# All seven products by blocks in the last two chunks of a fused attention and SwiGLU kernel

## The chip, the cores and the metric

The kernel runs on one core of a Trainium2 chip. Five engines work side by side, each with its own queue of instructions that it takes in order: TensorE (PE, with its weight loads shown apart as PEld), VectorE (DVE), ScalarE (ACT), GpSimd (POOL), and SyncE (SP), which here only issues transfers. They wait for each other on semaphores. The metric is the device time of one execution in microseconds; lower is better.

## The reference

```python
scores = q @ k.T / sqrt(64)                       # 8 batches x 8 heads, 576 x 576
scores = where(scores >= max(scores) - tau, scores, -1e9)
attn   = softmax(scores);  x = attn @ v           # heads joined: x is 4608 tokens x 512
g, val = x @ w_gate, x @ w_val                    # 512 -> 1536, both
out    = (g * sigmoid(g) * val) @ w_out           # 1536 -> 512
```

All of it is float32.

## The kernel before

**Order.** The program is written out by a planner when it is built (class `Plan`, from line 30). `pe()` appends to TensorE's queue at once, in the order in which the Python code calls it. Work for the other engines is a `job` with an engine, an assumed duration, what it depends on and a rank; the planner places jobs into each engine's queue by the time at which it believes they can start, the lower rank first. So the order within each queue is fixed in the program, by assumed durations; on the chip the semaphores alone decide the times.

**Chunks.** The FFN takes the tokens in nine chunks of 512. Chunk c below 8 is the first 512 tokens of batch c; chunk 8 (`B` in the code) is the last 64 tokens of all eight batches, collected in `last_hbm`. In the *main part* there are 84 slots of attention scores (L1989) with softmax and the attends (L2088); the FFN work of earlier chunks is put between them. Behind the last scores and attends comes the *tail* (from L2321, `tail[0] = True`): chunk 7's gates, chunk 7's outputs, chunk 8's gates, chunk 8's outputs, one after the other.

**Gates and values.** For one chunk the products with `w_gate` and `w_val` are made in six groups g of 256 columns each. In a group, a two-by-two scheme of Winograd's kind replaces eight products by seven, p1 to p7, each of a sum of weight blocks and a sum of token blocks; the results are combined by adds. `Group` (L1092) makes each product with four matmuls of 128x128 weights by 256 tokens (`mul`, L1109). The weights' sums were made once and lie in `sums_hbm`, nine pieces of 512 columns per group, and `load_flow` (L1030) brings a group's pieces into one of two slots, in two transfers of 1280 and 1024 KB, for each chunk anew. `NestedGroup` (L1276) makes two of the seven products, p5 and p3, *by blocks*: the same scheme once more inside the product, seven matmuls of 128x128 by 128 tokens in place of four by 256 (L1294). Such a product leaves seven blocks in two PSUM banks (512 and 384 columns), which have to be copied out and folded by four adds (`Seven.fill` at L1214 and L1216, `Seven.fold`, `fold_banks` at L1233). It also needs four further sums of weights (the pieces 0 and 8 of `sums_hbm`) and four further sums of token blocks (`deepen_x`). In the main part some groups are nested; in the tail all are.

**After the products.** p1's result is copied within PSUM by ACT (`cb`, L1116), so that p2 adds to the one copy and p6 to the other. p6's result goes through ACT to a buffer u1 (L1155), to which p3's is added: the gate for one half. p7's and p5's give the other. `finish` takes a tanh (L1163, ACT), multiplies by the value (L1164, DVE), and multiplies by the gate into `hall`. This last multiply and some sums are POOL's in the main part (helper line L925) and DVE's in the tail (helper line L928).

**Outputs.** `Deep` (L1641) makes the products with `w_out`, nested by blocks (L1711, 21 matmuls each; in the tail some flat ones, L1720). It needs sums of the gated values: `early`, `late` and `inner_sums`; results come through `combine` (L1748 and helper adds) and are stored.

**Weights' slots.** SP issues every load in its queue's order; a load that waits for a slot to be free holds up the ones behind it.

## Time and profile before

| | |
|---|---|
| median of 3 runs (lowest to highest) | 1350.09 us (1348.88 to 1350.68) |
| the profiled execution: its own time | 1349.87 us |
| its span | 1348.0 us |
| granted TensorE clock, mean | 1.00 |
| busy: PE / DVE / ACT / POOL | 1334.6 / 1066.5 / 895.7 / 778.0 us |
| last attends of the main part's scores on TensorE | 1126.1 us |
| tail's gates begin | 1135.6 us |
| HBM read / written | 172.36 MB / 27.13 MB |

The profile's rows name a line of the kernel, an engine, an operation, out<-in by the program's names, the tile's shape, the count, then the busy time in us, the mean of one in ns, and after the bar the idle time ahead of these instructions with what ended it. A float32 matmul stands in the trace as two records, so the counts of PE rows are twice those of the code. `tmp`, `big`, `hall`, `vall`, `pall`, `tall`, `xall`, `obs`, `qT` and `kT` are SBUF tiles, `pa`, `pb`, `pe`, `sc`, `px` and `py` PSUM banks. `big` is a large tile with many uses, weights' slots among them.

### The profile page before, as it was taken

Reading aid. Unit: us, or ns where it says so; the run is one execution under the profiler, and the core shown is the slowest. Engines: PE = TensorE matmul, PEld = TensorE weight load, DVE = VectorE, ACT = ScalarE, POOL = GpSimd, SP = SyncE. Lnnn points to the kernel's source line nnn. Section 1 sums busy time; section 2 is a strip of 40 time slices with the busy share of each in tenths; the row PEclk is TensorE's granted clock in tenths of the full one; section 3 lists DMA queues with packets and bytes.
Section 4 is the critical chain, followed back from the end, with each engine's and each line's share of the span. In section 5 each row is a group of like instructions: output and inputs, shape, how many; then the busy total and the mean of one; then the engine's idle time right before and its main releaser. Section 6 shows DMA issues by size and latency. Waiting matters only on the chain.

```text
span 1348.0 us, 40299 instructions
## 1 busy us (share of the span) xinstructions
PE 1334.6 (99%) x15914; PEld 1118.9 (83%) x15914; DVE 1066.5 (79%) x2860; ACT 895.7 (66%) x2315; POOL 778.0 (58%) x870
## 2 busy tenths in 40 slices
PE   9999999999999999999999999999999999999998
PEld 7777777787888878888888888887888889999998
DVE  7888898888887777888788888888788876586686
ACT  6888777767756677787777777778677773330330
POOL 2677497565685659745994689566965594000000
PEclk9999999999999999999999999999999999999999
DMA  8753324356557543746264636562565518524621
GB/s 178 206 186 96 79 58 133 122 149 177 153 166 225 169 126 92 211 137 203 62 201 145 216 97 195 158 215 69 139 212 145 171 57 270 195 96 165 210 80 32
DMA packets 216140, 202.11 MB, mean 150 GB/s; under 512 B 166800, under 2 KB 184208, under 8 KB 205200
## 3 DMA queue, kind: packets, MB, share of 16 engines
q1 hardware_dynamic: 212032, 198.62, 50.0%
q8 instruction: 126, 2.06, 0.6%
q10 hardware_dynamic: 3920, 0.92, 0.3%
q14 instruction: 62, 0.51, 0.1%
HBM read 172.36 MB, written 27.13 MB: 148 GB/s over the span
## 4 chain that ended last, share of the span: by engine, by line
PE 93%; DVE 2%; DMA 2%; POOL 1%; ACT 1%; issue 1%; SPq 0%; ACTq 0%; DVEq 0%; POOLq 0%
PE pb L1109 19%; PE pa L1109 13%; PE px L1711 12%; PE sc L1989 10%; PE xa L2088 9%; PE pe L1109 6%; PE po L1416 6%; PE pe L1294 4%; PE py L1711 3%; PE pv L1341 2%; PE pg L1341 2%; PE sc L1294 2%; PE py L1720 2%; PE sc L483 1%; PE pv L600 1%; DMA wo<-in_moe_w_gate_dram 1%
## 5 line engine op out<-in xcount | busy, mean ns | idle before, releaser
L2037 DVE SCALAR_TENSOR_TENSOR pall<-sc,th,pall 128x288 f32<-128x288 f32 x504 | 244.3, 513 | 42.0 <-ACT pall L2035 22.6
L1109 PE MATMUL pb<-xall,big 128*128 128x256 f32 x1152 | 273.9, 381 | 0.0
L2035 ACT ACTIVATE pall<-sc,nm 128x288 f32<-128x288 f32 x504 | 232.8, 498 | 33.6 <-DVE pall L2037 33.5
L1109 PEld LDWEIGHTS pb<-xall,big 128*128 128x128 f32 x1152 | 214.9, 190 | 30.7 <-issue 2.7
L2066 DVE STREAM_TRANSPOSE pall<-pall 128x576 f32<-128x576 f32 x252 | 188.4, 764 | 23.6 <-ACT pall L2064 15.6
L2064 ACT ACTIVATE pall<-pall,ri 128x288 f32<-128x288 f32 x388 | 179.0, 527 | 28.4 <-DVE ri L2052 27.5
L1109 PE MATMUL pa<-xall,big 128*128 128x256 f32 x768 | 183.1, 381 | 0.0
L925 POOL TENSOR_TENSOR hall<-hall,tmp 128x512 f32<-128x512 f32 x80 | 102.2, 1280 | 106.5 <-DVE hall L1164 86.0
L1109 PEld LDWEIGHTS pa<-xall,big 128*128 128x128 f32 x768 | 143.2, 190 | 21.7 <-issue 2.5
L2010 DVE TENSOR_REDUCE mx<-sc 128x2 f32<-128x576 f32 x168 | 125.9, 750 | 43.4 <-PE sc L1989 42.8
L925 POOL TENSOR_TENSOR big<-big 128x128 f32<-128x128 f32 (+3 forms) x174 | 129.1, 750 | 44.1 <-ACT big L1216 22.3
L1989 PE MATMUL sc<-kT,qT 64*32 64x288 f32 (+1 forms) x5376 | 144.7, 345 | 1.0 <-DVE pall L2037 1.0
L1989 PEld LDWEIGHTS sc<-kT,qT 64*32 64x32 f32 x5376 | 95.1, 106 | 50.0 <-issue 9.3
L2088 PE MATMUL xa<-pall,vall 64*32 64x288 f32 x4032 | 128.8, 404 | 0.4 <-PE px L1711 0.4
L2088 PEld LDWEIGHTS xa<-pall,vall 64*32 64x32 f32 x4032 | 75.4, 107 | 46.1 <-issue 4.3
L2061 POOL TENSOR_SCALAR pall<-pall,ri 128x288 f32<-128x288 f32 x116 | 58.7, 518 | 71.8 <-DVE ri L2052 70.0
L1109 PE MATMUL pe<-xall,big 128*128 128x256 f32 x384 | 91.4, 381 | 0.0
L2046 ACT COPY sums<-sums 32x6 f32<-32x6 f32 x336 | 66.6, 198 | 30.2 <-DVE pall L2037 26.1
L1163 ACT ACTIVATE vall<-tmp 128x512 f32<-128x512 f32 x96 | 59.9, 627 | 36.8 <-POOL tmp L925 17.3
L1109 PEld LDWEIGHTS pe<-xall,big 128*128 128x128 f32 x384 | 72.4, 190 | 11.1 <-ACT pall L2064 1.1
L2012 DVE TENSOR_REDUCE mx<-sc 128x1 f32<-128x288 f32 x168 | 75.0, 446 | 0.0
L925 POOL TENSOR_TENSOR big<-hall 128x384 f32<-128x384 f32 (+2 forms) x69 | 65.2, 969 | 14.6 <-PE pa L1109 14.5
(290 smaller groups left out, 2629.5 us busy)
## 6 DMA issues: line engine op xcount, KB each, us to landing
big<-sums_hbm SPq DMA_DIRECT2D x42, 1280.0 KB, 6.7
big<-sums_hbm SPq DMA_DIRECT2D x42, 1024.0 KB, 6.9
vall<-in_v_dram SPq DMA_DIRECT2D x112, 144.0 KB, 3.6
sums_hbm<-big SPq DMA_DIRECT2D x36, 256.0 KB, 3.6
out_dram<-big SPq DMA_DIRECT2D x32, 256.0 KB, 3.0
qT<-in_q_dram SPq DMA_DIRECT2D x112, 72.0 KB, 4.0
kT<-in_k_dram SPq DMA_DIRECT2D x112, 72.0 KB, 3.1
wo<-in_moe_w_gate_dram SPq DMA_DIRECT2D x16, 384.0 KB, 3.7
```

The costliest lines, as they stand in the source:

```text
L925: return lambda: nc.gpsimd.tensor_tensor(out=out, in0=a, in1=b, op=op)
L1109: nc.tensor.matmul(ps[:, i], w[:, k_, i * P:(i + 1) * P], x[:, k_, :], start=first and i == k_ == 0, stop=True, skip_group_check=True)
L1294: nc.tensor.matmul(self.es[b_].ap()[:, at_ * P:(at_ + 1) * P], ws[n], xd[o][n], start=b_ not in begun, stop=True, skip_group_check=True)
L1416: nc.tensor.matmul(ps, h(f), w[:, f, :], start=(f == 0), stop=(f == NF2 - 1))
L1711: nc.tensor.matmul(ps, a[:, f, :], ws[n][:, f, :], start=bank_ not in begun, stop=True, skip_group_check=True)
L1989: nc.tensor.matmul(pss[h][(slice(g * G, (g + 1) * G), *part)], qT[hs, col:col + G], kT[hs, c * SH + keys[0]:c * SH + keys[1]], start=True, ...
L2010: rs.append(job("DVE", 0.72, lambda n=n, tile_=tile_: nc.vector.tensor_reduce(out=mx[:, n:n + 2, 0], in_=tile_[:, :, 0:SH], axis=AX.X, op= ...
L2035: ej = job("ACT", 0.42, lambda x=x, n=n: nc.scalar.activation(ps[x], scs[x], AF.Exp, bias=nm[:, n:n + 1]), ej, masks.get((h, u - 1)), rank=0)
L2037: masks[x] = job("DVE", 0.45, lambda x=x, n=n: nc.vector.scalar_tensor_tensor(out=ps[x], in0=scs[x], scalar=th[:, n:n + 1], in1=ps[x], op0 ...
L2064: scaled.append(job("ACT", 0.46, lambda x=x, n=n: nc.scalar.activation(x, x, AF.Copy, scale=ri[:, n:n + 1]), rj, rank=rank))
L2066: seg["turned"].append(job("DVE", 0.72, lambda both=both: nc.vector.transpose(out=both, in_=both), *scaled, rank=rank))
L2088: nc.tensor.matmul(holds[a].ap()[x * G:(x + 1) * G, 0:SH].rearrange("d (i q) -> d i q", q=G), vr[rs, h, j, ds], p[rs, h, :, j, :], start=( ...
```

## The change

In the main part the change adds `store_more`: in each of chunks 2 to 6, for each of the six groups, the four further weight sums of one more product (`MORE`: the chunk, and which product) are made from the slot in which that product's weights lie for the chunk's own use. POOL makes them for groups 0 to 4, DVE for group 5; the place is a part of `hall` that is not in use then, and one store of 256 KB brings them to `more_hbm`. The next load into that slot waits for these adds (`load_flow`), and the gated values of group 5 wait for the store (`finish`). In chunk 6's outputs some ranks change.

In the tail, `NestedGroup` is replaced by class `Whole`: all seven products of every group by blocks, for chunk 7 and chunk 8 in turn, group by group: (7,0), (8,0), (7,1) and so on. Weights lie in ten cells of 512 KB (`load_cell`, two transfers of 256 KB each); each of the 42 cells is loaded once and read by both chunks. `deepen_all` makes the token sums for all seven operands of both chunks, on DVE for three of them and on POOL for four. Four pairs of PSUM banks hold the products. The folds of the gate and the value side's inner sums are POOL's; p2's and p4's results are folded by one ACT copy and four DVE adds (`folded`). Chunk 8's gated values are stored to `hall_hbm` and loaded again as four quarters behind the gates; then come the outputs of chunk 7 and of chunk 8, one directly behind the other.

TensorE's order up to the tail's gates is the same in both programs. In the tail it has 588 matmuls of 128x128 by 128 in `product` for what were 240 by 256 and 168 by 128; the output products are the same in number.

```diff
+    MORE = {2: 0, 3: 1, 4: 3, 5: 6, 6: 4}
+    more_reads, more_stores, more_of_place = {}, {}, {}
+
+    def more_place(g, n):
+        at_ = list(MORE.values()).index(n) * HW
+        return more_hbm[g][:, at_:at_ + HW]
+
+    def store_more(c, g):
+
+        n = MORE[c]
+        if (c, g) in more_reads or (c, g, n // 4) not in loads:
+            return
+        w = flow_part(g % 2, n + 1)
+        place = hall[:, g % 2, NF2 - 1]
+        a11, a12, a21, a22 = (w[:, k_, i * P:(i + 1) * P] for i in range(2) for k_ in range(2))
+        t2, t4, t3, t1 = (place[:, k_, i * P:(i + 1) * P] for i in range(2) for k_ in range(2))
+        deps = loads[c, g, n // 4], more_of_place.get((c, g % 2))
+        tt, eng, took, rank = (pool_tt, "POOL", 0.46, 3) if g < NF2 - 1 else (dve_tt, "DVE", 0.25, 2)
+        j = job(eng, took, tt(t3, a11, a21, ALU.subtract), *deps, rank=rank)
+        j = job(eng, took, tt(t1, a21, a22, ALU.add), j, rank=rank)
+        j = job(eng, took, tt(t2, t1, a11, ALU.subtract), j, rank=rank)
+        more_reads[c, g] = j = job(eng, took, tt(t4, a12, t2, ALU.subtract), j, rank=rank)
+        more_of_place[c, g % 2] = more_stores[g, n] = job("SP", 0.1, lambda: nc.sync.dma_start(
+            out=more_place(g, n).rearrange("p (k f) -> p k f", k=2), in_=place), j, lag=2.0, moves=1.3)
...
+        before = (c, g - 2) if g >= 2 else (c - 1, g + NF2 - 2)
+        if before in more_reads and lo <= MORE[before[0]] + 1 < to:
+            deps = *deps, more_reads[before]
...
+                mv = mv, more_of_place.get((self.c, t))
...
+    def load_cell(N, *deps):
+        if N >= NQ * NF2:
+            return
+        g, n = N // NQ, J[N % NQ]
+        place = cell(N)
+        deps = *deps, stores[g], *plain_stores[g], *nested_stores[g]
+        base = job("SP", 0.5, lambda: nc.sync.dma_start(out=place[:, 0:HW], in_=sums_hbm[g][:, (n + 1) * HW:(n + 2) * HW]),
+                   *deps, lag=1.6, moves=0.9)
+        if n in (2, 5):
+            more = sums_hbm[g][:, 0:HW] if n == 2 else sums_hbm[g][:, (NS_ - 1) * HW:]
+            cell_loads[N] = base, job("SP", 0.5, lambda: nc.sync.dma_start(out=place[:, HW:], in_=more), *deps, lag=1.6, moves=0.9)
+            return
+        cell_loads[N] = base, job("SP", 0.5, lambda: nc.sync.dma_start(out=place[:, HW:], in_=more_place(g, n)), more_stores[g, n], *deps,
+                                  lag=1.6, moves=0.9)
...
+            rank = min(rank, 1) if tail[0] else rank
+            if self.c == B - 1 and not self.in_outputs:
+                tt, eng, took = pool_tt, "POOL", 1.3
-            rank = 0 if o == 1 else 1 if o == 5 or o in (3, 6) and not tail[0] else 2
+            tt, eng, took = (dve_tt, "DVE", 0.55) if tail[0] else (pool_tt, "POOL", 1.0)
+            rank = 0 if o == 1 else 1 if o == 5 or o in (3, 6) and not tail[0] or o in (0, 6) and tail[0] or self.c == B - 2 else 2
...
-                tt, eng, took, less, rank = dve_tt, "DVE", 0.42, 0.29, 0
+                tt, eng, took, less, rank = dve_tt, "DVE", 0.42, 0.29, -1 if self.c == B - 2 else 0
...
-            if self.c < B:
+            if self.c < B - 2:
                 load_flow(self.c + 1, g, part, *deps)
+
+        def free_cells(self, *ks_and_deps):
+            if self.c == B - 2:
+                ks, *deps = ks_and_deps
+                for N in sorted((k_ - FIRST_CELL) % NCELL for k_ in ks):
+                    load_cell(N, *deps)
...
+            if c in MORE:
+                store_more(c, g)
...
+    deps = [j for js in ready_x[B - 1].values() for j in js]
+    deepen_all(B - 1, "DVE", -1, 0, 1, 1, fourths[0][:, 0:1], *ready_x[B - 1][0], attended, last=deps)
+    deepen_all(B - 1, "DVE", -1, 2, 2, 2, fourths[0][:, 1:3], *deps, attended)
+    for n, o in enumerate((5, 6, 1, 3)):
+        deepen_all(B - 1, "POOL", 0, o, 1, 1, fourths[1][:, n:n + 1], *deps, attended)
+    x11, x21, x12, x22, s1, s2, s4 = (bases[B][:, n * HW:(n + 1) * HW] for n in range(NQ))
+    free = [j for b in n_list for j in b.jobs]
+    j1 = job("DVE", 0.62, dve_tt(s1, x21, x22, ALU.add), *last_x, rank=0)
+    j2 = job("DVE", 0.62, dve_tt(s2, s1, x11, ALU.subtract), j1, rank=0)
+    j3 = job("DVE", 0.62, dve_tt(x21, x11, x21, ALU.subtract), j2, rank=0)
+    deepen_all(B, "DVE", 0, 0, 1, 1, None, j3, *free)
+    j4 = job("DVE", 0.62, dve_tt(s4, x12, s2, ALU.subtract), j3, rank=0)
+    deepen_all(B, "DVE", 0, 2, 2, 2, None, j4, x_ready[B, 0])
+    for o in (5, 6, 1, 3):
+        deepen_all(B, "POOL", 0, o, 1, 1, None, j4, *free)
...
+        def product(self, n, both, first, *deps):
+            begun = set() if first else {0, 1}
+            N = NQ * self.g + J.index(n)
+            w, more = (cell(N)[:, x * HW:(x + 1) * HW].rearrange("p (k f) -> p k f", k=2) for x in range(2))
+            a11, a12, a22 = w[:, 0, 0:P], w[:, 1, 0:P], w[:, 1, P:2 * P]
+            t2, t4, t3, t1 = (more[:, k_, i * P:(i + 1) * P] for i in range(2) for k_ in range(2))
+            ws, xd = (a11, a12, t4, a22, t1, t2, t3), x_sets[self.c, X_OF[n]]
+
+            def fn():
+                for x in ORDER:
+                    b_, at_ = AT[x]
+                    nc.tensor.matmul(both.ap(b_)[:, at_ * P:(at_ + 1) * P], ws[x], xd[x], start=b_ not in begun, stop=True,
+                                     skip_group_check=True)
+                    begun.add(b_)
+
+            m = pe(NEST, fn, *deps, *cell_loads[N], x_ready[self.c, X_OF[n]])
+            if self.c == B:
+                load_cell(N + NCELL, m)
+            return m
...
+        def p1(self):
+            self.a = Both("pa")
+            m = self.product(0, self.a, True, *self.a.deps)
+            a, b = self.a, Both("pb", full=True)
+            self.b = b
+            self.cb = [job("ACT", (0.57, 0.46)[x], lambda x=x: nc.scalar.copy(b.ap(x), a.ap(x)), m, *b.deps, rank=0) for x in range(2)]
+
+        def p5(self):
+            self.e = Both("pe")
+            m = self.product(2, self.e, True, *self.e.deps)
+            self.s, _ = s7s[0], s7s.rotate(-1)
+            self.c5 = self.s.fill(self.e.holds, m, 0)
...
+            j = job("ACT", 0.28, lambda: nc.scalar.copy(y[:, 4:5], q0[:, 0:1]), m, *st.jobs, rank=0)
+            j = job("DVE", 0.42, dve_tt(y[:, 0:2], twice(y[:, 4:5]), q0[:, 1:3], ALU.add), j, rank=0)
+            j = job("DVE", 0.42, dve_tt(y[:, 3:5], twice(y[:, 1:2]), q1[:, 1:3], ALU.add), j, rank=0)
+            j = job("DVE", 0.29, dve_tt(y[:, 1], y[:, 3], q0[:, 3], ALU.add), j, rank=0)
+            j = job("DVE", 0.42, dve_tt(y[:, 2:4], twice(y[:, 4:5]), q1[:, 0:2], ALU.add), j, rank=0)
+            both.done(j)
...
+        def p6(self):
+            m = self.product(3, self.b, False, *self.cb)
+            self.u, _ = u1s[0], u1s.rotate(-1)
+            self.u1 = self.u.fill(self.b.holds, m, 0)
...
+            tj = job("ACT", 0.6, lambda: nc.scalar.activation(two(n.ap), u.ap, AF.Tanh), gj, *n.jobs, rank=0)
+            o = st.ap[:, 0:DM]
+            vj = job("DVE", 0.75, lambda: nc.vector.scalar_tensor_tensor(out=o, in0=n.ap, scalar=1.0, in1=o, op0=ALU.add, op1=ALU.mult),
+                     tj, fj, rank=0)
+            n.jobs = [vj]
+            eng = ENDS[c][t]
+            tt, took = (dve_tt, 0.62) if eng == "DVE" else (pool_tt, 1.3)
+            to = hall[:, t, g] if c < B else two(o)
+            mj = job(eng, took, tt(to, two(o), u.ap, ALU.mult), vj, rank=0)
+            u.jobs = [mj]
...
+            last_stores[t, g] = job("SP", 0.5, lambda: nc.sync.dma_start(out=hall_hbm[t, h][:, x * HW:(x + 1) * HW], in_=o), mj,
+                                    lag=2.0, moves=0.9)
...
+            js = [job("DVE", (0.7, 0.55)[x], lambda x=x: nc.vector.scalar_tensor_tensor(
+                out=u[:, x * 4 * P:(4, 7)[x] * P], in0=e.ap(x), scalar=0.5, in1=u[:, x * 4 * P:(4, 7)[x] * P], op0=ALU.mult, op1=ALU.add),
+                m, *self.u1, rank=0) for x in range(2)]
+            e.done(*js)
+            j = self.u.fold(GATE_FOLDS[self.c][0], 0, *js)
+            self.finish(0, self.u, j, self.st, self.fa)
...
+            m = self.product(6, self.b, False, *self.u1)
+            b, s_ = self.b, self.s.place
+            self.u2 = [job("DVE", (0.7, 0.55)[x], lambda x=x: nc.vector.scalar_tensor_tensor(
+                out=s_[:, x * 4 * P:(4, 7)[x] * P], in0=b.ap(x), scalar=0.5, in1=s_[:, x * 4 * P:(4, 7)[x] * P], op0=ALU.mult, op1=ALU.add),
+                m, *self.c5, rank=0) for x in range(2)]
+            self.g2 = self.s.fold(GATE_FOLDS[self.c][1], 1, *self.u2)
+
+        def p4(self):
+            m = self.product(4, self.b, False, *self.u2)
+            st, j = self.folded(self.b, m)
+            self.finish(1, self.s, self.g2, st, j)
...
+    old = None
+    for g in range(NF2):
+        for c in (B - 1, B):
+            new = Whole(c, g)
+            new.p1()
+            if old is not None:
+                new.p5()
+                old.p4()
+            if (c, g) == (B - 1, NF2 - 1):
+                state["deep"] = Deep(B - 1, plan.t + plan.PIPE)
+                state["deep"].early(plan.t + plan.PIPE, True)
+            for fn in (new.p2, new.p6, new.p3, new.p7) if old is not None else (new.p5, new.p2, new.p6, new.p3, new.p7):
+                fn()
+                if (c, g) == (B, NF2 - 1) and fn == new.p2:
+                    state["deep"].late(plan.t + plan.PIPE)
+                if (c, g) == (B, NF2 - 1) and fn == new.p6:
+                    state["deep"].sixth_sums(plan.t + plan.PIPE)
+            old = new
+    state["last_product"] = old.p4
+    begin_outputs(B - 1)
+    out_steps(2)
+    behind = plan.t + plan.PIPE
+    used = [j for b in (*u1s, *s7s, *stages, *n3) for j in b.jobs]
+    for x in ob_jobs[0:2]:
+        x += s7s[0].jobs + s7s[1].jobs + s7s[2].jobs
+    stream(5, True, behind)
+    stream(3, True, behind, *used)
+    for n in range(4):
+        t, h = divmod(n, 2)
+        j = job("SP", 0.1, lambda n=n, t=t, h=h: nc.sync.dma_start(out=last_quarters[n].rearrange("p f n -> p (f n)"), in_=hall_hbm[t, h]),
+                *(last_stores[t, h * (NF2 // 2) + x] for x in range(NF2 // 2)), behind, *used, lag=2.0, moves=2.6)
+        for x in range(NF2 // 2):
+            gated[B, t, h * (NF2 // 2) + x] = j
...
+    final = Deep(B, plan.t + plan.PIPE)
+    out_steps(1)
+    final.in_outputs = True
+    final.early(plan.t + plan.PIPE)
+    while state["run"]:
+        out_steps(1)
+    state["deep"] = final
+    begin_outputs(B)
```

More of the change, by code (lines that the diff above doesn't have):

```diff
@@ L1168, in finish @@
             hold.done(True)
-            tt, eng, took = (dve_tt, "DVE", 0.62) if tail[0] else (pool_tt, "POOL", 1.3)
+            tt, eng, took = pool_tt, "POOL", 1.3
             gated[self.c, t, self.g] = mj = job(eng, took, tt(ht, ht, gb.ap, ALU.mult), vj, rank=rank)
@@ L1676, in late @@
             self.ready["s1"].append(self.sum(self.a21, self.a21, self.a22, ALU.add, n - 1, j3[n - 1], gated[c, 1, NF2 - 1], rank=1))
[L1677 removed]
+            self.ready["s2"] = [self.sum(self.s2, self.a22, self.s3, ALU.subtract, x, j3[x], gated[c, 1, n + x], mark, self.read[1], rank=1) for x in range(n)]
         def sum(self, out, a, b, op, x, *deps, rank=2):
@@ L2159, in gates_and_values @@
         old = None
-        settled[0] = c >= DEEP and not tail[0]
+        settled[0] = c >= DEEP
         while u_bufs[0] is not u_list[0]:
@@ new lines, with __init__, free_at, ap @@
+    class Pair:
+        def __init__(self, banks_, full):
+            self.banks, self.full, self.held = banks_, full, False
+        def free_at(self):
+            return max(b.free_at() for b in self.banks)
+    class Both:
+        def __init__(self, name, full=False):
+            free = [p for p in pairs if not p.held and (p.full or not full)]
+            few = sum(p.full for p in free) == 1 and not full
+            self.pair = min(free, key=lambda p: (p.full and few, max(p.free_at(), plan.t)))
+            self.pair.held = True
+            self.holds = [Hold(b, name) for b in self.pair.banks]
+            self.deps = [d for h in self.holds for d in h.deps]
+        def ap(self, n):
+            return self.holds[n].ap()[:, 0:(4, 3)[n] * P]
+        def done(self, *jobs):
+            for h in self.holds:
+                h.read_by(*jobs)
+                h.done(True)
+            self.pair.held, self.pair.full = False, True
@@ new lines, with seven, plain @@
+    mine = [h.bank for h in state["deep"].x]
+    rest = [b for b in banks if b.fixed is None and b not in mine]
+    others = [b for b in banks if b.fixed is not None]
+    pairs = [Pair(mine, True), Pair(rest, False), Pair(others[0:2], False), Pair(others[2:4], False)]
+    def seven(place, *jobs):
+        b = Seven(place)
+        b.jobs = list(jobs)
+        return b
+    def plain(place, *jobs):
+        b = Buf(place)
+        b.jobs = list(jobs)
+        return b
+    old_tall = [behind, *(j for b in (*u_list, *s_bufs) for j in b.jobs)]
```

233 lines of the change are left out of this document (148 added, 85 removed).

## The prediction

> **What bounds the kernel now.** I read the page's busy shares and slices first, then the chain that ended last, then TensorE's waits, then stretches of the span, then the timeline of the stretch at which the change begins to alter TensorE's order.
>
> ```profile
> PE 1334.6 (99%) x15914; PEld 1118.9 (83%) x15914; DVE 1066.5 (79%) x2860; ACT 895.7 (66%) x2315; POOL 778.0 (58%) x870
> POOL 2677497565685659745994689566965594000000
> PE 93%; DVE 2%; DMA 2%; POOL 1%; ACT 1%; issue 1%; SPq 0%; ACTq 0%; DVEq 0%; POOLq 0%
> ```
>
> TensorE is busy 99% and is 93% of the chain: only fewer TensorE microseconds, or a new stall, can move the time. POOL does nothing in the last six slices. The stretches (time, length, then busy and count of PE, PEld, DVE, ACT, POOL, then clock, DMA share, GB/s):
>
> ```profile
> 500.00:700.00 200.00, 200.00 (x2869) 169.25 (x2875) 162.40 (x468) 148.93 (x405) 156.34 (x171) 1.00 0.52 151
> 1150.00:1200.00 50.00, 50.00 (x291) 45.61 (x290) 33.23 (x67) 18.27 (x34) 0.00 (x0) 1.00 0.51 174
> 1300.00:1348.00 48.00, 44.49 (x321) 41.99 (x320) 33.99 (x69) 6.62 (x14) 0.00 (x0) 0.99 0.09 23
> ```
>
> Main part and tail both run with TensorE full. The only waits that TensorE shows after 130 us are of 1.0, 0.6 and 0.4 us. Now the timeline at the start of the tail's gates; each product of four 128x256 matmuls (x8, two records for each) is on L1109, one of seven 128x128 matmuls on L1294:
>
> ```profile
> 1130.79 1.60 PE L1711 MATMUL px<-wo,hall 128*128 128x128 f32 x12
> ...
> 1135.58 1.89 PE L1109 MATMUL pa<-xall,big 128*128 128x256 f32 x8
> 1137.31 0.61 PE L1294 MATMUL pe<-xall,big 128*128 128x128 f32 x4
> ...
> 1138.87 1.89 PE L1109 MATMUL pa<-xall,big 128*128 128x256 f32 x8
> 1140.60 1.89 PE L1109 MATMUL pb<-xall,big 128*128 128x256 f32 x8
> ```
>
> Start to start, a product of four takes 1.73 us (1138.87 to 1140.60) and one by blocks 1.56 (1137.31 to 1138.87; 1.556 over many). That is 0.432 and 0.2225 per matmul.
>
> **The change on TensorE.** Until the gates of the tail TensorE's order stays, instruction for instruction. In the tail, 60 products (five of seven in six groups of two chunks, 240 matmuls) become products by blocks (420 more of 128x128): 60 x (1.73 - 1.556) = 10.4 us less. The output products stay. The tail before has no stall: 240 x 0.432 + 168 x 0.2225 + 210 x 0.2235 + 48 x 0.432 = 208.8, and 1135.58 + 208.8 = 1344.4, where the last product in the trace ends (it starts at 1339.14 and takes 5.34). After: 588 x 0.2225 + 46.9 + 20.7 = 198.4.
>
> One rule speaks against halving the columns. The Trainium skill, "TensorE: Matmul & The Clock Gate", section "Back-to-back issue gap", gives about 81 ns for a 128-column matmul with its weight load and 131 for one of 512; put evenly between, 256 columns cost 98, and a product by blocks would cost 7 x 81 against 4 x 98, 1.45 times, some 47 us more in all. The trace disagrees: it is 0.90 times.
>
> **What the tail's other engines must do.** A group takes 7 x 1.556 = 10.89 us. The rows are of the tail for ACT and VectorE (DVE), of the main part for POOL and for the last line:
>
> ```profile
> L1214 ACT ACTIVATE vall<-sc 128x384 f32<-128x384 f32 x12 | 5.9, 491 | 19.7 <-PE sc L1294 19.7
> L1216 ACT ACTIVATE vall<-pe 128x512 f32<-128x512 f32 x8 | 4.8, 597 | 0.0
> ...
> L928 DVE TENSOR_TENSOR hall<-hall,tmp 128x512 f32<-128x512 f32 x24 | 16.6, 692 | 0.8
> L928 DVE TENSOR_TENSOR big<-big,sc 128x256 f32<-128x256 f32 x30 | 12.6, 420 | 4.1 <-ACT big L1233 3.3
> ...
> L925 POOL TENSOR_TENSOR big<-big 128x256 f32<-128x256 f32 x52 | 37.7, 728 | 29.3 <-ACT big L1216 22.3 <-ACT sums L2046 3.8 <-DVE nm L2028 1.1
> L925 POOL TENSOR_TENSOR big<-big 128x128 f32<-128x128 f32 x64 | 29.3, 459 | 11.2 <-PE pe L1109 6.6 <-DMA sums_hbm<-big 0.8
> L925 POOL TENSOR_TENSOR hall<-hall,tmp 128x512 f32<-128x512 f32 x80 | 102.2, 1280 | 106.5 <-DVE hall L1164 86.0 <-DVE hall L1362 11.7 <-ACT pall L2064 5.3
> ...
> L928 DVE TENSOR_TENSOR tmp<-tmp,big 128x512 f32<-128x512 f32 x11 | 9.6, 873 | 0.0
> ```
>
> - ACT: three pairs of PSUM copies (512 and 384 wide, about 1.07 each), two corner copies (0.27), two tanh (0.63): 5.0 of 10.89.
> - DVE: two folds out of PSUM (2 x 1.55), two scaled sums of 512 + 384 (2 x 1.24), two gated multiplies and one end multiply (3 x 0.69): 7.7 of 10.89.
> - POOL: two folds (3 x 0.73 + 0.46 = 2.65 each) and one end multiply (1.28): 6.6 of 10.89. Chunk 7's output sums (11.5 us) fall into the last two groups, 13.2 + 11.5 against 21.8, but the products that read the last of them begin 5 us later.
>
> So no engine is full, and the loops' extra buffers (two or three of each) span a whole group. What is left is latency. Three places are tight. (1) p6's result is copied by ACT in two pieces before p7, with only p3 between: a like pair ended 1.18 us after the next product's start (1243.24 to 1244.42), 0.38 short of 1.556; ACT's queue has the second tanh right ahead of it. That tanh waits for POOL's second fold: gate fold from 0 to 2.7 us after p7's end, second to 5.4, tanh to 6.0, and p6's copy is due at 7.8; 1.8 us to spare. (2) VectorE's sums of x for chunk 8 are ready about when its second product wants them. (3) POOL's first sums for chunk 7. I cost the steady groups at nothing, since ACT and POOL have these margins; the bound from above is 0.5 us in each of 12 groups, 6 us.
>
> **The start of the tail.** Here I find a real stall. By VectorE's new order the block sums of x for the first p5 stand partly behind the combine of the last output block (four adds, 1.73, from 1136.13 when ACT has copied the corner). Interleaved with two 0.43 adds of x, p5's operand is done at 1137.9 where TensorE wants it at 1137.14: 0.8 us. Then p2 waits for the copies of p1 into the second pair, which that combine frees at 1138.6; two copies (0.57 + 0.49) end at 1139.7, where p2 could start at 1139.5: 0.3 us. POOL's sixteen 0.46 us adds after the token sums (1134.0) end at 1141.4, about when p6 and p3 want the first of them. I take 1.1 us for the start and 0.8 for places 2 and 3 together (bounds 0 and 2). The sum is 1.9.
>
> **Main part.** Added are 30 groups of four 128x128 adds: 25 on POOL (4 x 0.46 = 1.84, 46 us in all) and 5 on VectorE (4 x 0.29, 6 us), and 30 stores of 256 KB on SP. Over chunks 2 to 6 that is 9.2 us of POOL in some 140: from 78% (156 of 200) to 85%. SP and DMA (52%, 151 GB/s) gain 7.7 MB over 700 us, 11 GB/s. New waits: the next load into a weight slot waits for the adds that read it; queued behind it on SP are loads of q, k, v and stores; who waits in the end is a product two groups later. On POOL an add waiting for its weights holds up the end multiplies and output sums behind it. Also the last output block of chunk 6 now waits for sums that POOL takes later. TensorE does not stall from 140 to 1125 us, so POOL's present lateness is all hidden. Bounds: 0 and 46 us (each added POOL microsecond reaching TensorE); the nearest row is POOL's own 22% idle with no TensorE wait, so I take 0.
>
> **Loads in the tail.** 84 halves of 256 KB replace 24 loads of 1.0 to 1.3 MB; bytes fall from 27.6 to 22 MB, for 131 us: 168 GB/s, against 174 now. A cell is asked for ten products (15 us) ahead, and loads of 1 MB landed in 6.9 us; SP's issues are in order, each waiting for its product. Chunk 8's gated values go out (12 stores) and come back in four loads behind the last store; then two more rounds of sums on VectorE. Asked for some 14 us into chunk 7's outputs, landed 8 us later, sums 7 us: 29 of the 33.8 that these outputs take. Hidden, by 5 us.
>
> **Sum.** The profiled execution took 1349.87 (span 1348.0 and 1.87 around it; the median of the runs is 0.22 more). 1349.87 - 10.4 + 1.9 = 1341.4; I say 1341.5.
>
> **Rivals.**
> - Small stalls each group (place 1): POOL and VectorE get in each other's way. For it: the same kind of add with two SBUF inputs takes 692 in the tail with POOL idle and 873 beside POOL. Then POOL's folds, with three such operations of VectorE in a group, grow by up to 3 x 0.69 = 2.1 us, and 1.8 us to spare turns into a 0.3 us stall; with a slow copy 0.5 x 12: 1347.5. Against: each stall lengthens the group and gives POOL time, and half the operations miss each other. The Trainium skill, "SBUF — State Buffer", section "Who interferes with whom", calls this a lock that one side holds for a whole instruction; the 181 ns in the mean are a quarter of that, so the trace shows it in part.
> - Chunk 8's quarters come late, by 10 us instead of 5 early: 5 us, 1346.5. For: SP is in order behind the output stores. Against: the margin.
> - Slower: POOL in the main part. At the ends of chunks it is 95 to 100% busy for some 45 of 140 us. If an added group stands there, output sums move back by 1.84 us; from 1.7 of the 9.2 us per chunk on (8.5 over five chunks) the gain is gone, and with half of it (23 us) the time is 1364. For: waits of POOL on loads in a fixed order. Against: TensorE has no stall to show how near it is.
> - The gain isn't there: seven small matmuls limited by weight loads. Against: L1294 already runs at 0.2225 us beside 0.432.
>
> **Chances.** Forecast 0.66 (1339.6 to 1344); stalls by group 0.13 (to 1348); late quarters 0.07 (to 1347); POOL in the main part 0.13 (a third below 1347, the rest above 1350); no gain 0.01. A difference below 0.2% (2.7 us) is about what a measurement of this kernel cannot tell from none. Faster is then 0.83, same 0.05, slower 0.12. The range from 1339.3 (no stall at all) to 1348 leaves out the main part's bad cases and a little at either end.
>
> **What would show it.** Right: the tail's gates start at 1135.6 again; products start 1.556 us apart; a hole of about 1 us near 1138; POOL 60% busy from 1140 to 1270; the last product ends near 1336. Wrong: holes of TensorE released by POOL, or by the weights' DMA, between 300 and 1125; ACT's copy of p6 late behind a tanh; a hole before chunk 8's outputs.

## The result

| | before | changed |
|---|---|---|
| median (lowest to highest), 11 runs each | 1350.15 us (1348.88 to 1351.28) | 1346.53 us (1344.70 to 1348.23) |
| profiled execution, own time / span | 1349.87 / 1348.0 us | 1348.23 / 1346.4 us |
| TensorE busy | 1334.6 us | 1328.4 us |
| POOL busy | 778.0 us | 935.9 us |

The ratio is 0.9975, 95% interval 0.9966 to 0.9984: faster by 3.6 us, where 8.6 were forecast. The profiled execution of the changed kernel happens to be the slowest of its eleven, 1.7 us above its median; what its parts cost is read from it, and its sum is compared with its own time.

The page of the changed kernel, busy times and POOL's slices:

```profile
PE 1328.4 (99%) x16274; PEld 1122.4 (83%) x16274; DVE 1083.5 (80%) x2887; ACT 896.5 (67%) x2341; POOL 935.9 (70%) x1119
POOL 2578397565686759947895779666976699855910
```

POOL now works through the tail's gates, and 9 us more in the stretch of 200 us that was shown of before. The stretches of the changed kernel (columns as before):

```profile
500.00:700.00 200.00, 200.00 (x2834) 169.55 (x2840) 166.53 (x476) 148.97 (x405) 165.49 (x192) 1.00 0.54 162
1150.00:1200.00 50.00, 49.47 (x443) 49.27 (x442) 31.36 (x69) 20.94 (x46) 35.99 (x53) 1.00 0.61 190
1250.00:1300.00 50.00, 48.18 (x397) 46.80 (x396) 41.83 (x68) 13.25 (x29) 34.21 (x33) 1.00 0.27 93
```

TensorE, which had no gap in the tail before, has 0.5 us of gap in the second row and 1.8 in the third. Its waits after 130 us name who made them:

```profile
PE sc L1755 <- DVE hall L929: 1.8, 2, 1.3
PE sc L2045 <- DVE pall L2093: 0.6, 1, 0.6
PE pg L1371 <- ACT big L568: 0.6, 1, 0.6
PE pe L1333 <- ACT big L1273: 0.6, 1, 0.6
PE pe L1333 <- DVE hall L1197: 0.6, 1, 0.6
PE pb L2532 <- ACT tmp L1273: 0.5, 1, 0.5
```

The second and third of these stand at 140.7 and 134.6 us; the kernel before has the like of them (1.0 and 0.6). Because TensorE's order is the same up to the tail, each of its instructions can be set against its twin. That gives the account of the two profiled executions:

| stretch of TensorE | before | changed | difference |
|---|---|---|---|
| start to 139.6 us | 139.61 | 140.68 | +1.07 |
| from there to the tail's first gate product (1135.58 / 1139.46) | 995.97 | 998.78 | +2.81 |
| tail, first gate product to the start of the last flat output product | 203.56 | 197.96 | -5.60 |
| from there to the end of the span | 8.90 | 9.01 | +0.11 |
| span | 1348.04 | 1346.42 | -1.6 |

The first row has nothing to do with the change (last section). The other two are what has to be explained: 2.8 us lost in the main part, where I took 0, and 5.6 gained in the tail, where I took 8.5.

**Where the main part loses.** From 140 to 871 us the twins stay together. Then TensorE waits twice in one group, and once more each near 882 and 1026. TensorE at 871:

```profile
870.56 0.71 PE L1333 MATMUL pe<-xall,big 128*128 128x128 f32 x4
871.83 0.49 PE L1333 MATMUL pe<-big 128*128 128x128 f32 x2 [0.56 <-DVE hall L1197]
873.05 1.89 PE L1138 MATMUL pb<-xall,big 128*128 128x256 f32 x8
875.51 0.71 PE L1333 MATMUL pe<-xall,big 128*128 128x128 f32 x4 [0.57 <-ACT big L1273]
```

The first wait is for a PSUM bank that VectorE's gated multiply frees; that multiply waited for a tanh, and the tanh for POOL:

```profile
870.42 0.63 ACT L1196 ACTIVATE vall<-tmp 128x512 f32<-128x512 f32 x1 [3.87 <-POOL tmp L926]
871.09 0.69 DVE L1197 SCALAR_TENSOR_TENSOR hall<-vall,pb 128x512 f32<-128x512 f32 x1 [3.28 <-ACT vall L1196]
```

POOL in the changed kernel, then in the kernel before:

```profile
857.72 0.75 POOL L2191 TENSOR_SCALAR qT<-qT,scl 128x576 f32<-128x576 f32 x1
865.98 0.87 POOL L926 TENSOR_TENSOR hall<-big 128x128 f32<-128x128 f32 x2 [7.52 <-DMA big<-sums_hbm]
866.93 0.46 POOL L926 TENSOR_TENSOR hall<-hall,big 128x128 f32<-128x128 f32 x1
867.47 0.46 POOL L926 TENSOR_TENSOR hall<-big,hall 128x128 f32<-128x128 f32 x1
867.88 1.27 POOL L926 TENSOR_TENSOR hall<-hall,tmp 128x512 f32<-128x512 f32 x1
869.11 1.28 POOL L926 TENSOR_TENSOR tmp<-tmp,big 128x512 f32<-128x512 f32 x1
```

```profile
863.38 1.27 POOL L925 TENSOR_TENSOR hall<-hall,tmp 128x512 f32<-128x512 f32 x1 [6.09 <-DVE hall L1164]
864.61 1.28 POOL L925 TENSOR_TENSOR tmp<-tmp,big 128x512 f32<-128x512 f32 x1
```

The four adds of `store_more` stand ahead of the end multiply and of the inner sum (`tmp<-tmp,big`). POOL sits idle for 7.5 us waiting for the weights to land, does the adds, and only then the two operations that TensorE needs: 4.5 us later than before, 3.4 of them beyond the 1.1 us by which all of this execution runs later. In this group TensorE loses 1.7 us (its distance to the twin goes from 1.1 to 2.8 us), and 0.6 us each near 882 and 1026. These two smaller losses I did not follow to one instruction; all of them are gone in the kernel without the adds (experiment 5).

**Where the tail loses.** Two places carry most of it. Between them, from 1180 to 1250, TensorE has no wait, and POOL's folds take 2.75 us each. At 1169, POOL, then ACT, then TensorE:

```profile
1163.57 1.27 POOL L926 TENSOR_TENSOR hall<-big,xall 128x512 f32<-128x512 f32 x1 [0.63 <-DVE big L2584]
1164.80 3.63 POOL L926 TENSOR_TENSOR big<-big 128x256 f32<-128x256 f32 x4
```

```profile
1168.46 0.63 ACT L2582 ACTIVATE qT<-big 128x512 f32<-128x512 f32 x1 [1.81 <-POOL big L926]
1169.00 0.47 ACT L1271 ACTIVATE tmp<-pb 128x384 f32<-128x384 f32 x1
1169.37 0.59 ACT L1273 ACTIVATE tmp<-pb 128x512 f32<-128x512 f32 x1
```

```profile
1170.01 0.71 PE L2532 MATMUL pb<-xall,big 128*128 128x128 f32 x4 [0.54 <-ACT tmp L1273]
```

The fold takes 3.63 us where I had 2.65; the tanh that waits for it stands ahead of the copy of p6 in ACT's queue, and p7 starts 0.7 us late. And at the start of chunk 7's outputs (the 42 records of this product take 7.35 us, where 4.69 is the usual):

```profile
1277.80 0.83 PE L1755 MATMUL sc<-big,hall 128*128 128x128 f32 x6
1279.05 0.94 PE L1755 MATMUL sc<-wo,hall 128*128 128x128 f32 x6 [0.41 <-DVE hall L929]
1280.04 1.60 PE L1755 MATMUL sc<-big,hall 128*128 128x128 f32 x12
1282.99 0.94 PE L1755 MATMUL sc<-wo,hall 128*128 128x128 f32 x6 [1.35 <-DVE hall L929]
```

TensorE waits for VectorE's second inner sums:

```profile
1278.18 2.40 DVE L929 TENSOR_TENSOR hall<-hall 128x384 f32<-128x384 f32 x3
1281.43 1.51 DVE L929 TENSOR_TENSOR hall<-hall 128x384 f32<-128x384 f32 x1
```

The last of them takes 1.51 us, where such an add took 0.55 in the tail before. VectorE's rows between 1155 and 1276 say why VectorE is late:

```profile
L929 DVE TENSOR_TENSOR pall<-pall,sc 128x256 f32<-128x256 f32 x21 | 8.7, 413 | 0.0
L2584 DVE SCALAR_TENSOR_TENSOR big<-kT,big 128x512 f32<-128x512 f32 x8 | 6.8, 849 | 10.6 <-ACT kT L2582 10.5
L929 DVE TENSOR_TENSOR big<-big 128x384 f32<-128x384 f32 x4 | 4.2, 1071 | 0.0
L2604 DVE SCALAR_TENSOR_TENSOR big<-sc,big 128x384 f32<-128x384 f32 x6 | 3.3, 546 | 0.0
```

An add of 384 with both operands in SBUF takes 1071 ns beside POOL, 552 in the tail before, when POOL was idle; one with an operand in PSUM (`sc`) is unchanged: 413 against 420 for 256 columns, and 546 for 384 columns in both kernels. The Trainium skill, "SBUF — State Buffer", section "Who interferes with whom", states this split: a VectorE instruction with two SBUF inputs contends with a POOL instruction that reads SBUF, and one with at most one SBUF input (outside the two-port modes) does not. The trace agrees, by these rows.

### The profile page after: what moved, and what is told of

It is laid out like the page before. It is cut to its first block, busy times and chain, and to the rows that moved or that the text cites. A ratio compares the mean times of both kernels' runs of the same rounds, so it can differ in the third digit from the quotient of the medians.

```text
span 1346.4 us, 41681 instructions
## 1 busy us (share of the span) xinstructions
PE 1328.4 (99%) x16274; PEld 1122.4 (83%) x16274; DVE 1083.5 (80%) x2887; ACT 896.5 (67%) x2341; POOL 935.9 (70%) x1119
## 5 line engine op out<-in xcount | busy, mean ns | idle before, releaser
L1138 PE MATMUL pb<-xall,big 128*128 128x256 f32 x864 | 205.8, 381 | 0.0
L926 POOL TENSOR_TENSOR big<-big 128x128 f32<-128x128 f32 (+3 forms) x214 | 158.0, 747 | 36.0 <-ACT big L1273 12.4
L1138 PEld LDWEIGHTS pb<-xall,big 128*128 128x128 f32 x864 | 161.2, 190 | 24.0 <-issue 2.7
L1138 PE MATMUL pa<-xall,big 128*128 128x256 f32 x576 | 137.7, 382 | 0.0
L1138 PEld LDWEIGHTS pa<-xall,big 128*128 128x128 f32 x576 | 107.8, 190 | 17.5 <-issue 2.5
L926 POOL TENSOR_TENSOR big<-hall 128x384 f32<-128x384 f32 (+2 forms) x72 | 70.5, 1002 | 14.2 <-PE pa L1138 14.0
L926 POOL TENSOR_TENSOR hall<-hall 128x384 f32<-128x384 f32 (+2 forms) x70 | 71.6, 1036 | 0.9
```

Of the source, the lines that this page charges most:

```text
L926: return lambda: nc.gpsimd.tensor_tensor(out=out, in0=a, in1=b, op=op)
L1138: nc.tensor.matmul(ps[:, i], w[:, k_, i * P:(i + 1) * P], x[:, k_, :], start=first and i == k_ == 0, stop=True, skip_group_check=True)
```

## The experiments

Lateness of the main part means, for TensorE, the growth of the distance to its twin in the kernel before between 139.6 and 1135 us. "Tail" is the third row of the account above.

| kernel | main part late by | tail | median | ratio to before, interval |
|---|---|---|---|---|
| changed | 2.8 | 198.0 | 1346.53 | 0.9975 (0.9966 to 0.9984) |
| adds late | 3.6 | 198.3 | 1349.05 | 0.9993 (0.9984 to 1.0002) |
| second sums first | 3.8 | 197.7 | 1347.32 | 0.9985 (0.9975 to 0.9995) |
| no adds (a write waits in their place) | 22.6 | 198.0 | 1366.45 | 1.0120 (1.0105 to 1.0135) |
| folds as writes | 1.8 | 193.9 | 1342.58 | 0.9947 (0.9930 to 0.9964) |
| no adds, no wait | 0.2 | 197.8 | 1344.70 | 0.9957 (0.9940 to 0.9973) |
| folds as writes, twice | 1.6 | 195.6 | 1343.94 | 0.9953 (0.9938 to 0.9968) |
| adds planned later | 0.8 | 197.3 | 1346.28 | 0.9972 (0.9960 to 0.9984) |
| end multiplies on VectorE | 3.8 | 199.5 | 1349.19 | 0.9996 (0.9987 to 1.0006) |
| changed, again | 3.8 | 198.2 | 1347.58 | 0.9981 (0.9972 to 0.9990) |
| later + second sums first | 0.9 | 197.3 | 1344.53 | 0.9958 (0.9946 to 0.9971) |
| later + folds planned slower | 1.1 | 200.3 | 1346.55 | 0.9977 (0.9967 to 0.9987) |
| all three | 0.8 | 200.3 | 1347.64 | 0.9977 (0.9968 to 0.9986) |

Five of these have the changed kernel's main part word for word (both with folds as writes, second sums first, ends on VectorE, and the repeat); their lateness is 1.6 to 3.8 us, so one trace gives it to about 1 us only. Six have the changed kernel's tail word for word (changed, adds late, the two without adds, adds planned later, and the repeat): 197.3 to 198.3 us, so a difference below 1 us in the tail says nothing either.

**1. The adds asked for later.**

```diff
-            if c in MORE:
-                store_more(c, g)
...
-                if c in MORE and fn == new.p2:
-                    store_more(c, g + 1)
+                if c in MORE and fn == (new.p2 if MORE[c] < 4 else new.p7):
+                    store_more(c, g, plan.t + plan.PIPE)
```

> The four adds of store_more are asked for later: for a product of the first load behind p2 of its own group, for one of the second load behind p7, when the weights have surely landed. TensorE's order is unchanged. Theory A (in the changed kernel an add on GpSimd waits for its weights' load, idle for 7.5 us, and holds up the end multiply and the inner sum behind it; TensorE is 2.8 us late by that between 139 and 1135 us): the tail's gates begin 2 to 2.8 us sooner than in the changed kernel, time about 1344. Rival B (GpSimd's added 46 us are simply too much, wherever they stand): no gain, 1346.5. Rival C (the next weights' load, which waits for these adds, now comes late): slower, 1348 or more.

Here the adds of group 5 (and of group 4 in chunks 5 and 6) are asked for behind the place where the outputs' sums look for them, so some read weights that are already written over. Measured: no gain. The waits at 871 are gone, but 1.7 us are lost before 958 and again by 1104, each where the attends wait for VectorE's gated multiply. The cost only moved. Theory A's size is not confirmed by this, nor B's; the edit was too coarse.

**2. The second sums first.**

```diff
-            rank = 0 if o == 1 else 1 if o == 5 or o in (3, 6) and not tail[0] or o in (0, 6) and tail[0] or self.c == B - 2 else 2
+            rank = -1 if o == 1 and self.c == B - 1 else 0 if o == 1 else 1 if o == 5 or o in (3, 6) and not tail[0] or o in (0, 6) and tail[0] or self.c == B - 2 else 2
```

> Only a rank: the second inner sums of chunk 7's outputs, for which TensorE waits 0.4 and 1.35 us at 1279 and 1283, are put ahead of other work of VectorE that is ready at the same time. If the hole is an order in VectorE's queue, it shrinks by 0.4 to 1.5 us (1345 to 1346). If VectorE's queue is late as a whole, because its instructions take longer beside GpSimd, the hole stays within 0.3 us (1346.5).

The wait within chunk 7's second output product falls from 1.8 us to 0.4, as a matter of order in VectorE's queue. But 1.7 us appear before chunk 8's outputs, behind VectorE's L1909, where 0.3 stood: the tail is 0.3 shorter, not 1.4, and that is within the spread of the tail. VectorE as a whole is late there.

**3. No adds, first try.**

```diff
-        j = job(eng, took, tt(t3, a11, a21, ALU.subtract), *deps, rank=rank)
...
-        more_reads[c, g] = j = job(eng, took, tt(t4, a12, t2, ALU.subtract), j, rank=rank)
+        j = clear_first(place, *deps)
+        more_reads[c, g] = j
```

> The four adds of each store_more are left out (one tiny write of VectorE stands for them); the 30 stores and all waits of loads stay. The tail reads these weights, so this leaves out a part of the computation. Theory A and rival B both say: the 2.8 us of the main part go, the tail's gates begin near 1136.6 and the time is about 1343.7. If instead the 30 stores, the loads behind them in SyncE's queue or the changed ranks of chunk 6's outputs were the cause, the main part stays as late as it is: 1346.5.

The small write of VectorE that I put in the adds' place keeps their wait for the weights. Three times, at the seams near 511, 655 and 800 us, TensorE loses 7 to 8 us: 20 us more than the changed kernel, with less work. The releaser is not shown there, and I did not follow it; for the question of the adds the run is unusable, and both expectations are missed.

**4 and 6. The tail's folds as writes of zeros.**

```diff
+            if tail[0] and eng == "POOL":
+                tt = lambda out, a, b, op: (lambda: nc.gpsimd.memset(out, 0.0))
```

and for the second kernel each write twice:

```diff
+                tt = lambda out, a, b, op: (lambda: [nc.gpsimd.memset(out, 0.0) for _ in range(2)])
```

> In the tail GpSimd's folds are writes of zeros into the same places, so that GpSimd reads nothing there while it still writes (this leaves the folds out). If VectorE and GpSimd get in each other's way by reads from SBUF, VectorE's operations with two SBUF operands that stand beside these writes go back to the 0.69 (512 wide) and 0.55 us (384 wide) of the tail before (in the changed kernel up to 1.06 and 1.07), and the holes of TensorE at 1169 (0.7) and 1278 to 1283 (2.7) shrink by more than half: about 1344. If any work of GpSimd slows VectorE, the durations stay as they are.

> As the kernel whose folds in the tail are writes of zeros (the folds are left out), but each write is made twice, so that GpSimd is busy nearly as long as with the folds (2 x 0.31 us for one 256 wide, against 0.73) and still reads nothing. If the lock between VectorE and GpSimd is what makes the folds late, the tail from its first product to the start of the last flat product takes 194 to 195 us, as with single writes (193.9), in place of 198.0. If it was GpSimd's time alone, it goes back to 196.5 to 198.

With single writes the tail takes 193.9 us and no wait of TensorE above 0.15 is left in it. So the products by blocks, without the folds' cost, give 203.56 - 193.91 = 9.65 us; the folds on POOL take 4.05 back. But a write is short, 0.31 us against 0.73. With two of them POOL is busy for 2.3 us a fold, against 2.65 undisturbed, and reads nothing: 195.6, between the two expectations. VectorE's rows of that kernel:

```profile
L2586 DVE SCALAR_TENSOR_TENSOR big<-kT,big 128x512 f32<-128x512 f32 x8 | 5.5, 687 | 10.6 <-ACT kT L2584 10.5
L929 DVE TENSOR_TENSOR big<-big 128x384 f32<-128x384 f32 x4 | 3.8, 980 | 0.0
L929 DVE TENSOR_TENSOR hall<-hall 128x384 f32<-128x384 f32 x3 | 1.6, 552 | 0.0
```

Gated multiplies beside writes are back at 687 ns (849 beside folds). Of the four adds with a mean of 980, the two that still are slow (1.20 and 1.62 us) stand beside POOL's 512 wide output sums, which do read; the two beside writes take 0.54 and 0.56. So of the 4.05 us some 2.4 go with POOL's reads and some 1.6 with the time POOL needs; the second is a little low, as two writes are shorter than one add.

**5. No adds, and nothing in their place.**

```diff
-        j = job(eng, took, tt(t3, a11, a21, ALU.subtract), *deps, rank=rank)
...
-        more_reads[c, g] = j = job(eng, took, tt(t4, a12, t2, ALU.subtract), j, rank=rank)
+        more_reads[c, g] = None
...
-            out=more_place(g, n).rearrange("p (k f) -> p k f", k=2), in_=place), j, lag=2.0, moves=1.3)
+            out=more_place(g, n).rearrange("p (k f) -> p k f", k=2), in_=place), lag=2.0, moves=1.3)
```

> The four adds of each store_more are left out with their waits; nothing stands in an engine's queue for them. The 30 stores stay and write what lies in that place (so the weights of the tail are not the right ones). Theory A (the adds, with what they wait for and hold up): TensorE's lateness between 139 and 1135 us falls from some 3 us to below 0.7, and the time by 2 to 3 us against the changed kernel. Rival D (the stores, or the changed ranks of chunk 6's outputs): it stays at 2 to 4 us.

Lateness 0.2 us: it is the adds with what they wait for and hold up. The 30 stores and the changed ranks (rival D) cost nothing that can be seen. Whether it is the adds' work or their place, this run does not tell; the next one does. POOL in the stretch shown above does the end multiply at once again:

```profile
864.39 1.27 POOL L926 TENSOR_TENSOR hall<-hall,tmp 128x512 f32<-128x512 f32 x1 [6.10 <-DVE hall L1197]
865.62 1.27 POOL L926 TENSOR_TENSOR tmp<-tmp,big 128x512 f32<-128x512 f32 x1
```

**7. The adds planned later.**

```diff
-        deps = loads[c, g, n // 4], more_of_place.get((c, g % 2))
+        deps = job("none", 0.0, lambda: None, loads[c, g, n // 4], lag=4.0), more_of_place.get((c, g % 2))
```

("none" is an engine that exists only in the planner and emits nothing)

> The planner is told that each weights' load lands 4 us later for these adds alone, so they are put further back in GpSimd's and VectorE's queues; all else is the change. Theory A: GpSimd's idle time for the weights' load ahead of these adds (21.5 us in seven waits) falls below 8 us, TensorE's lateness in the main part falls from some 3 us to about 1, time 1344.5 to 1345. Rival B (wherever they stand they move other work of GpSimd back): the lateness stays above 2.5 us.

The adds are the same, 46 us of POOL, but behind the operations that TensorE needs. POOL's wait for the weights' load is no longer among its longest (21.5 us in seven waits in the changed kernel), and the main part is late by 0.8. The three kernels below that have this edit too are late by 0.8 to 1.1, against 1.6 to 3.8 in the six with the changed kernel's main part. So it was mostly the place in the queue, not the work: A, not B, with the reserve that the planner's other choices move a little with the adds (some places in VectorE's and ScalarE's queues change too). Nor is it rival C: the next load into the slot waits for these adds here too, and they are done later. The median is 1346.28, though; against the changed kernel, measured on another chip, the gain cannot be told.

```profile
867.68 0.88 POOL L926 TENSOR_TENSOR hall<-big 128x128 f32<-128x128 f32 x2
868.64 0.46 POOL L926 TENSOR_TENSOR hall<-hall,big 128x128 f32<-128x128 f32 x1
869.24 1.28 POOL L926 TENSOR_TENSOR hall<-hall,tmp 128x512 f32<-128x512 f32 x1
```

This is POOL in that kernel: three adds behind the two urgent operations (865.22 and 866.45), and the fourth behind the next one.

**8. Both end multiplies on VectorE.**

```diff
-    ENDS = {B - 1: ("DVE", "POOL"), B: ("DVE", "POOL")}
+    ENDS = {B - 1: ("DVE", "DVE"), B: ("DVE", "DVE")}
```

> The second end multiply of each group in the tail goes from GpSimd (1.28 us) to VectorE (0.69). GpSimd's folds then start up to 1.2 us sooner, and the hole at 1169 (0.7 us) should close; VectorE has one more operation with two SBUF operands in a group (8.4 of 10.9 us). If GpSimd's lateness makes the holes: tail 1 to 2 us shorter than 198.0. If VectorE is the tighter one there (it is behind before chunk 7's outputs): the hole at 1278 grows, tail 198 to 200.

Tail 199.5: VectorE is the tighter one. The hole at 1169 closes, but the waits for VectorE before the outputs grow to 3.6 us in all (`px` 2.5, `sc` 1.1).

**9 to 12. Combinations, beside the changed kernel on one chip.**

> The changed kernel itself, as the measure for the three beside it on one chip. Its main part should again be 2 to 4 us late, by GpSimd's adds, its tail 198 us, with the same holes at 1169 and 1278 to 1283; time 1346 to 1347.5.

It is late by 3.8 us in the main part and has the same holes in a tail of 198.2.

> The adds planned 4 us later, and the second inner sums of chunk 7's outputs first. If both causes are as read, the main part is late by 1 and the hole before chunk 7's second output product is 0.4 in place of 1.8: 1 to 3 us below the changed kernel beside it. If what VectorE does not do at 1278 is missed later (1.7 us before chunk 8's outputs, as with that rank alone), the gain is that of the adds alone, 1 to 2 us.

The adds planned later and the second sums first: 1344.53 us, 3.05 below the changed kernel's 1347.58 on the same chip, and 5.65 below before's 1350.18. In the profiled executions the main part is 2.8 us shorter than the repeat's and the tail 0.8. The adds planned later alone also had a tail of 197.3, so no gain of the second sums' rank is shown. It has the lowest median of the kernels here that leave nothing out. What is left in its tail: the 0.5 at p7, 0.4 within the second output product, and

```profile
1304.83 1.60 PE L1755 MATMUL px<-wo,xall 128*128 128x128 f32 x12 [1.37 <-DVE big L1909]
```

```diff
-            tt, took, less = (dve_tt, 0.36, 0.23) if eng == "DVE" else (pool_tt, 0.85, 0.52) if tail[0] else (pool_tt, 0.75, 0.44)
+            tt, took, less = (dve_tt, 0.36, 0.23) if eng == "DVE" else (pool_tt, 1.05, 0.62) if tail[0] else (pool_tt, 0.75, 0.44)
```

> The adds planned 4 us later, and the planner told that a fold of GpSimd in the tail takes 3.8 us in place of 3.1 (the trace has 3.3 to 3.7). Then ScalarE's queue has the second tanh behind the copy of p6. If that order made the hole at 1169, it closes (0.7 us), and the tail is 196.5 to 197.5. If GpSimd's lateness itself is the limit, another hole takes its place and the tail stays at 198.

> All three: adds planned later, folds planned at 3.8 us, second inner sums first. By theory A and the queue orders: main part late by 1, tail 195.5 to 196.5, time 2 to 4 us below the changed kernel beside it (1343 to 1345). By the rival that VectorE and GpSimd together are too slow at the end of the gates: tail 197.5 or more, 1345.

With a truer duration for the fold, the planner puts the tanh behind the copy of p6 and the hole at p7 closes. Two new ones take its place, both on VectorE; the waits of the first of these kernels:

```profile
PE px L1755 <- DVE big L929: 2.4, 3, 1.7
PE pe L2532 <- DVE big L929: 1.4, 1, 1.4
```

The tail is 200.3 with either. The planner's other durations (VectorE's adds beside POOL) were not changed with it, so its picture is no truer as a whole.

## Why the prediction was wrong

The forecast was 8.5 us off the tail and nothing lost in the main part. Measured in the profiled executions: 5.6 off the tail and 2.8 lost. Of the 2.9 missing in the tail, 0.75 is a saving put too high and 2.15 are stalls put too low.

- **TensorE's saving: right, a little large.** 10.4 us forecast, 9.65 measured without stalls. Products by blocks start 1.563 us apart (12 of them in a row, 1215.45 to 1234.21), against the 1.556 of my row. The rule that I weighed, by which such a product would cost 1.45 times one of four, does not hold for these float32 products: they cost 0.905 times one of four.
- **"So I take 0" for the main part: the step that failed.** I wrote the mechanism down (an add waiting for its weights holds up the end multiplies behind it) and then costed POOL's adds by its idle share, 22%. Idle time of an engine whose queue is in order was no room here: what counts is whether the operation behind the waiting one can wait. It cost 2.8 us in the profiled execution, 3.8 in its repeat, and 0.2 without the adds. The rival "POOL in the main part" named the place; it was priced as whole added groups (1.84 us each) or nothing, and half of it at 23 us.
- **The tail's stalls: the second step that failed; the sum was half of what came, and in other places.** Forecast 1.9, measured 4.05. The start, 1.1 forecast, cost 0.15: I let p5 wait for its last operand, but its seven matmuls wait one by one, and the late operand belongs to a later one. Place 1 cost 0.7 once, not in every group, through the tanh as described. What I missed is the 2.7 us within chunk 7's second output product. I counted POOL's 11.5 us of output sums there, and nothing for VectorE, which has its inner sums, the last gated multiplies and the folds out of PSUM at the same time.
- **"Grow by up to 2.1 us": the rival was right in kind, its bound held, but its place was wrong.** I put the growth on POOL's folds alone, and in each of the twelve groups. Between 1180 and 1250 the folds stay at 2.75 us; they grow to 3.3 to 3.6 near both ends of the gates. There it lengthens VectorE's adds as much, and these are many at the end.
- **Late quarters: hidden, as forecast, though asked for later.** The loads are issued at 1291.8, 21.6 us behind the start of chunk 7's outputs (1270.16), where I had 14; they land at 1298.2, and the first sums are done at 1300.4, 8 us before TensorE comes to chunk 8's outputs (1308.68). The 0.3 us that it waits there is for VectorE's L1909, in whose queue these sums and 3.6 us of waiting for the load stand ahead.
- **Signs.** The tail's gates begin at 1139.46, not 1135.6; the hole near 1138 is 0.15 us, not 1; POOL is 73% busy from 1140 to 1270, not 60%; the products' spacing is as forecast. Two signs of being wrong came: holes of TensorE in the main part with POOL behind them, and a copy of p6 late behind a tanh.
- Sign and wide range held; the range was drawn to take in the rivals' cases. The forecast's own band, 1339.6 to 1344, did not hold, and the forecast gain was more than twice the measured one.

## What to carry to other kernels

Before work is added to an engine because it is idle, look at what its queue holds behind the new instruction and at what the new instruction waits for: adds that waited 7.5 us for a load held up two operations by 3.4 us and cost TensorE 1.7, 2.8 with all such adds; a few places later in the queue all of them cost 0.8 to 1.1. Where one engine is to relieve another, price both with each other's operands: here adds with two SBUF operands took up to twice their time beside POOL in the mean (1071 ns against 552), and those with one operand in PSUM took no longer. And when one hole is closed, read which one opens: of the repairs tried here, four moved the wait and one removed it.

## What the runs showed that I had not expected

The first 20 us differ between executions, though all these kernels begin alike. In the profiled execution of the changed kernel TensorE's granted clock is 0.84 and 0.82 from 5 to 15 us, and 1.00 in that of before:

```profile
5.00:10.00 5.00, 3.10 (x14) 1.74 (x13) 2.23 (x8) 1.49 (x2) 0.48 (x1) 0.84 0.89 166
10.00:15.00 5.00, 5.00 (x23) 3.68 (x23) 3.35 (x9) 2.43 (x6) 0.00 (x0) 0.82 1.04 295
```

```profile
5.00:10.00 5.00, 3.67 (x18) 2.52 (x17) 2.87 (x9) 1.60 (x3) 0.48 (x1) 1.00 0.87 174
10.00:15.00 5.00, 5.00 (x28) 3.87 (x27) 4.36 (x10) 3.46 (x10) 0.00 (x0) 1.00 1.04 283
```

Five of the fourteen profiled executions show a clock of 0.77 to 0.89 there (the changed kernel, its repeat, and experiments 2, 6 and 7); at 30 us TensorE is 1.4 to 1.6 us behind the kernel before in these five, and at most 0.15 in the others. Waits up to 139.6 us change that again: by then the kernels tried here stand between 1.0 us before and 1.3 us behind the kernel before. Runs of the kernel before, too, have a mean clock of 0.997 to 1.000. An offset of 1.3 us is a third of the gain measured here, so a single profiled execution says little about a difference of 3 us.

A write by POOL (0.31 us for 128x256) leaves VectorE's two-operand work at its undisturbed 687 ns, where POOL's adds on the same places make it 849.
